# A hand-fed instruction list replaced by another search of the same list, in a fused attention and MLP layer

## The chip, the cores and the metric

The kernel runs on one core of one Trainium2 chip. The metric is the device time of one execution in microseconds (us). Lower is better. Three runs of the kernel before gave 302.27, 302.45 and 305.53, so the median is 302.45.

## The reference, cut to what matters

The input `A_x` has 2048 rows of 640 numbers in bf16. A layer norm, an attention and a residual are followed by a second layer norm, an MLP and another residual.

```python
def _A_ref(x, wq, wk, wv, wo, beta):          # H = 32 heads, Dh = 20, N = 4 segments, L = 512
    q, k, v = heads(x @ wq), heads(x @ wk), heads(x @ wv)       # [1, 32, 4, 512, 20]
    phi = lambda t: jnp.where(t > 0, t + 1.0, jnp.exp(t))
    for s in range(N):
        logits = einsum('bhqd,bhkd->bhqk', qs, ks) * Dh ** -0.5 + mask
        p = softmax(logits);  a_dot = einsum('bhqk,bhkd->bhqd', p, vs)
        pq = phi(qs);  num = einsum('bhld,bhde->bhle', pq, M)
        den = einsum('bhld,bhd->bhl', pq, z)[..., None] + 1e-06
        o = g * num / den + (1.0 - g) * a_dot
        pk = phi(ks)
        M = M + einsum('bhld,bhle->bhde', pk, vs);  z = z + pk summed over l
    return o @ wo

h  = x + _A_ref(layernorm(x), wq, wk, wv, wo, beta)
h2 = h + silu(layernorm(h) @ w1) @ w2         # w1 640 x 1728, w2 1728 x 640
```

## The kernel before, in words

The work is cut into four segments of 512 rows (0 to 3), and a segment into four blocks of 128 rows. All of it is declared as nearly 1,500 named tasks, and each task belongs to one engine. `Graph.schedule` walks a written list, the string `ORDER`, and hands the tasks to their engines in just that order. Every engine, and each of the two DMA-issuing queues (SyncE's, called SP here, and ScalarE's), then works in order. A task that has to wait holds up all that follows it on its engine. An entry is `name/engine:slots`: the engine letter (A ScalarE, D VectorE, G GpSimd, S SyncE) is given where there is a choice, and the slots are the buffers or PSUM banks it takes. `Tracker.add` derives the semaphore waits from reads and writes, buffers included. The list was made by a planner that has its own costs; only the finished list is in the kernel.

The names that the text uses, with the line that their instructions show in the profile:

- `x0`, `x1`, `x2`, `x4`, `x8`, `x12` (L577) load rows; `w_q`, `w_k0`, `w_w1_0` to `w_w1_4` and so on (L580) load weights; a `w_w1` part is 432 KB.
- `n1_st`, `n1_r`, `n1_ap` (L745, L760 to L766, L772): statistics, reciprocal root and application of the first layer norm of a block. Blocks 4 to 7 are segment 1.
- `n1_tp`, `n1_te` (L781, L790): the transpose of segment 0 by TensorE and its eviction by ScalarE. Later segments use DMA transposes, `n1_tr` (L796), issued by SyncE.
- `re_wq0` to `re_wk4` (L697, on ScalarE L695) copy the weights of q and k into a padded layout. These are copies in the head.
- `pr` and `qe` (L859, L867 or L868): a projection to q or k, and its eviction. In segment 0 each is done in two halves, `x` and `y`.
- `vt00` to `vt011` (L899): twelve small SBUF to SBUF transfers that gather head rows left over from the first five groups, so that groups 5 to 7 exist. Group 5 to 7 scores of segment 0 (`qk7x0` first) wait for all twelve.
- `qk`, `e`, `mk` (L936, L947, L958): scores on TensorE, their exponential on ScalarE, the causal mask on GpSimd. `av` and `oe` (L979, L994): probabilities times values, and the eviction; `tn` and `nm` (L1012, L1025 and L1027): transpose and division.
- `v` and `ve` (L824, L834 or L835): the value projection and eviction. `ex`, `pha`, `phb` (L874, L881, L887): the feature map. `kt` (L1093) and `mz` (L1101): transpose of the feature map by DMA, and the memory update.
- `ot`, `wo`, `rs` (L1154, L1162, L1170): transpose by DMA, output projection, residual. `h1`, `th`, `s` (L1197, L1206, L1212) and `h2`, `o` (L1239, L1252): the MLP. `out` (L1257) stores rows.
- `fill34`, `fill17`, `fill3` (L617): matmuls of zeros that only keep TensorE busy. `vpad0` and `vpad1` (L624, L625): GpSimd memsets of padding beside the values; `mt`, `mta`, `mtb`, `mm`, `mzc`: small GpSimd tasks that make masks.

Of the kernel before, what the change touches and what calls it, by code (L numbers as in the profile page):

```python
# [324 lines left out]
D = 640  # L325
# [50 lines left out]
n1_st8:6 e1yb2 mk1yb_0 n1_tr6 mk1yb_256 phb011 oe4x/A:1 qk7x0:0 e7x2:2 e7x0 mk7x_0 n1_tr7 v02:4 ve02/A tn4x:6 av1x:7
oe1x/D:1 n1_ap11:2 nm4x:0 mk7x_256 n1_r8/G n1_ap9:0 pha031:1 qk5x0:0 e5x2:0 v11:4 e5x0 mk5x_0 mk5x_256 qk6x0:0 e6x0:1
ve11/D:1 tn2x:7 av7x:6 oe7x/D:0 tn1x:4 nm1x:3 nm2x:1 e6x2 mk6x_0 fill3:5 av3x:5 oe3x/A:1 mk6x_256 tn7x:6 nm7x:2
qk0ya0:0 e0ya2:5 av5x:4 oe5x/D:0 mz00:5 ma00/D:0 mb00:0 e0ya0 kt01:1 tn3x:7 nm3x:1 av6x:6 oe6x/D:1 qk1ya0:2 e1ya2:0
tn5x:7 nm5x:3 tn6x:6 nm6x:0 ot1:0 phb031 ot0 e1ya0 n1_st10:0 n1_r10/D v10:0 ve10/A qk2ya0:4 e2ya0:2 av0y:2 oe0y/D:1  # L380
mz02:3 ma02/D:3 v12:0 ve12/D e2ya2 qk2yb0:2 e2yb0:1 n1_ap10:1 w_w2_0/S mb02:0 wo1:6 rs1 e2yb2 mk2yb_0 n2_st1:5
qk3ya0:0 e3ya2:3 wo0:4 mk2yb_256 tn0y:6 nm0y:1 rs0 n2_r1/G n2_ap1:3 kt04:0 n2_tr1:0 av1y:7 oe1y/D:0 e3ya0 qk4ya0:0
pr101:6 qe101/D:0 e4ya2:4 n2_st0:3 n2_r0/G v13:4 ve13/D e4ya0 pha101:2 ex101:2 n2_ap0:3 n2_tr0 qk3yb0:0 pr120:7
e3yb2:5 e3yb0 qk4yb0:2 w_w2_1/S e4yb2:0 e4yb0 mk4yb_0 mk3yb_0 mk4yb_256 mk3yb_256 qe120/D:0 ex120:0 phb101 pha120:0
av2y:6 pr100:0 qk5ya0:2 e5ya2:2 oe2y/D:1 qe100/D tn2y:7 nm2y:2 pr121:1 qe121/D pha121:0 pha100:0 e5ya0 n1_ap8:3
# [929 lines left out]
```

## Time and profile before

| What | Value |
|---|---|
| median of three runs | 302.45 us |
| profiled execution, its own time | 302.91 us |
| its span, first to last instruction | 301.2 us |
| granted clock, mean | 0.999 |
| TensorE matmuls busy | 291.1 us (97%) |
| VectorE busy | 222.4 us (74%) |
| ScalarE busy | 221.2 us (73%) |
| GpSimd busy | 140.5 us (47%) |
| HBM read, written | 10.41 MB, 2.62 MB |

The table adds up over very different stages. In the first ten microseconds all engines wait for loads. From 10 to 45 us segment 0 is brought up. From 45 us to about 260 us attention of one segment runs beside the MLP of the one before, and from 260 us on only the MLP of segment 3 is left. A busy share of an engine in the table is therefore an average and bounds nothing by itself.

### The profile page before, as it was taken

The page shows a single profiled execution, that of the slowest core. Times are in us where ns is not written, and L with a number is a line of the kernel's source. Part 1 is how long each engine was busy: PE and PEld are TensorE (multiplying, and loading weights), DVE is VectorE, ACT ScalarE, POOL GpSimd, SP SyncE. Part 2 cuts the span into 40 slices and gives each one's busy share as a digit, 9 for nine tenths or more (in the row PEclk, how much of TensorE's full clock was granted, in tenths as well). Part 3 has the DMA queues.
Part 4 walks back from the last instruction along what each step waited for, and adds up shares of the span by engine and source line. Part 5 has one row for each costly group of instructions (what it writes and reads, how often), then busy time and mean ns, then how long its engine had stood idle before and what let it go on. Part 6 is the DMA issues. An engine that isn't in the chain of part 4 may idle for free.

```text
span 301.2 us, 7561 instructions
## 1 busy us (share of the span) xinstructions
PE 291.1 (97%) x3027; PEld 172.6 (57%) x3027; DVE 222.4 (74%) x519; ACT 221.2 (73%) x315; POOL 140.5 (47%) x271
## 2 busy tenths in 40 slices
PE   8899699999999999999999999999999999999996
PEld 6675355454655555656644544566565457764574
DVE  5999788878559789889679885758847778735613
ACT  2998798999997999999679989886787840004500
POOL 4799632534645556754645446662774621200000
PEclk9999999999999999999999999999999999999999
DMA  7999525315473200361441300243120022330001
GB/s 258 362 359 135 96 58 131 89 22 168 83 91 88 59 20 10 51 94 26 100 137 39 71 14 20 39 86 77 46 65 24 2 44 46 87 87 2 0 30 59
DMA packets 48738, 24.66 MB, mean 82 GB/s; under 512 B 39168, under 2 KB 47616, under 8 KB 48704
## 3 DMA queue, kind: packets, MB, share of 16 engines
q1 hardware_dynamic: 46604, 21.64, 31.4%
q10 hardware_dynamic: 2100, 2.55, 3.0%
q8 instruction: 24, 0.39, 0.5%
q14 instruction: 10, 0.08, 0.1%
HBM read 10.41 MB, written 2.62 MB: 43 GB/s over the span
## 4 chain that ended last, share of the span: by engine, by line
PE 81%; DVE 6%; ACT 5%; DMA 3%; SPq 2%; issue 1%; POOL 0%; ACTq 0%; DVEq 0%
PE ps_all L1239 20%; PE ps_all L1197 18%; PE ps_all L859 12%; PE ps_all L1162 8%; PE ps_all L936 7%; PE ps_all L824 6%; PE ps_all L979 5%; ACT PT L947 3%; SPq L899 2%; DMA x_tok<-in_A_x_dram 2%; PE ps_all L1008 2%; PE ps_all L1101 2%; DMA w_sb<-w_sb 2%; PE ps_all L1012 1%; PE ps_all L1191 1%
## 5 line engine op out<-in xcount | busy, mean ns | idle before, releaser
L947 ACT ACTIVATE PT<-ps_all 128x1024 bf16<-128x1024 f32 (+1 forms) x168 | 157.0, 993 | 19.5 <-PE ps_all L936 15.9
L958 POOL TENSOR_SCALAR_AFFINE_SELECT PT<-PT 128x512 bf16<-128x512 bf16 x128 | 81.8, 648 | 58.8 <-ACT PT L947 56.2
L1239 PE MATMUL ps_all<-w_sb,sT 128*128 128x320 bf16 (+2 forms) x462 | 64.8, 295 | 0.0
L1197 PE MATMUL ps_all<-hT,w_sb 128*128 128x512 bf16 (+1 forms) x325 | 62.8, 337 | 0.0
L1206 ACT ACTIVATE th<-ps_all 128x512 f32<-128x512 f32 (+2 forms) x70 | 34.4, 516 | 35.4 <-PE ps_all L1197 27.2
L1239 PEld LDWEIGHTS ps_all<-w_sb,sT 128*128 128x128 bf16 x462 | 43.3, 98 | 18.2 <-issue 2.4
L1212 DVE SCALAR_TENSOR_TENSOR sT<-th,ps_all 128x512 bf16<-128x512 f32 (+2 forms) x70 | 38.1, 560 | 18.0 <-ACT th L1206 17.2
L1197 PEld LDWEIGHTS ps_all<-hT,w_sb 128*128 128x128 bf16 x325 | 29.9, 98 | 25.3 <-issue 2.4
L766 POOL TENSOR_TENSOR rst<-rst,eps_c 128x1 f32<-128x1 f32 x32 | 18.6, 582 | 26.6 <-DVE rst L760 24.8
L1252 DVE SCALAR_TENSOR_TENSOR x_tok<-ps_all,x_tok 128x640 bf16<-128x640 f32 (+3 forms) x18 | 13.4, 747 | 22.9 <-PE ps_all L1239 22.9
L745 DVE BATCH_NORM_STATS2 stt<-x_tok 128x6 f32<-128x320 bf16 x62 | 27.2, 484 | 2.9 <-DMA x_tok<-in_A_x_dram 2.6
L1162 PE MATMUL ps_all<-wo_sb,oT 128*128 128x320 bf16 x160 | 24.1, 299 | 0.4 <-DVE x_tok L1252 0.4
L979 PE MATMUL ps_all<-PT,Vx 128*32 128x256 bf16 (+3 forms) x576 | 23.3, 287 | 0.4 <-DVE Vx L835 0.4
L1053 POOL TENSOR_TENSOR otok<-on 128x320 bf16<-128x320 bf16 x24 | 19.3, 805 | 9.1 <-DVE on L1045 9.1
L868 DVE CAST QK<-ps_all 128x512 bf16<-128x512 f32 x24 | 16.4, 688 | 6.7 <-PE ps_all L859 6.3
L994 DVE TENSOR_SCALAR oTs<-ps_all,lsc 128x512 bf16<-128x512 f32 (+1 forms) x31 | 18.9, 624 | 2.7 <-PE ps_all L979 2.6
L1045 DVE TENSOR_TENSOR on<-ps_all,rd 128x640 bf16<-128x640 f32 x24 | 19.8, 824 | 0.8
L1162 PEld LDWEIGHTS ps_all<-wo_sb,oT 128*128 128x128 bf16 x160 | 14.9, 98 | 7.7 <-issue 2.4
L859 PE MATMUL ps_all<-xT,wkr 128*128 128x512 bf16 x75 | 18.7, 380 | 0.0
L824 PE MATMUL ps_all<-wv_sb,xT 128*128 128x320 bf16 x120 | 18.3, 299 | 0.3 <-ACT Vx L834 0.3
L859 PE MATMUL ps_all<-xT,wqr 128*128 128x512 bf16 x75 | 18.5, 380 | 0.0
L979 PEld LDWEIGHTS ps_all<-PT,Vx 128*32 128x32 bf16 x576 | 12.3, 96 | 10.3 <-issue 3.9
(88 smaller groups left out, 344.9 us busy)
## 6 DMA issues: line engine op xcount, KB each, us to landing
w_sb<-in_B_w_dram SPq DMA_DIRECT2D x5, 432.0 KB, 11.0
x_tok<-in_A_x_dram SPq DMA_DIRECT2D x3, 640.0 KB, 10.3
w_sb<-in_B_w_dram SPq DMA_DIRECT2D x3, 480.0 KB, 3.8
out_dram<-x_tok SPq DMA_DIRECT2D x9, 160.0 KB, 1.8
out_dram<-x_tok ACTq DMA_DIRECT2D x6, 160.0 KB, 1.9
sT<-in_A_wq_dram SPq DMA_DIRECT2D x1, 800.0 KB, 6.3
wo_sb<-in_A_wo_dram SPq DMA_DIRECT2D x1, 800.0 KB, 12.5
QKV<-QK SPq DMA_DIRECT2D x11, 72.0 KB
```

Source lines behind the costliest of these rows:

```text
L745: T.add(DV, lambda e, hh=hh: e.bn_stats(out=stt[:, s, 6 * hh:6 * hh + 6], in_=xb[:, 320 * hh:320 * hh + 320]), reads=R((xa, xsub)), writes ...
L824: fns.append(lambda e, c=c, hh=hh: e.matmul(bank(ps, hh)[:, 0:320], lhsT=xT_[:, c, 128 * i:128 * i + 128], rhs=wv_sb[:, c, 320 * hh:320 * ...
L859: fns = [lambda e, kc=kc: e.matmul(bank(ps)[:, lo:hi], lhsT=wt[:, kc, c, :], rhs=xT_[:, kc, lo:hi], start=(kc == 0), stop=(kc == NC - 1)) ...
L936: fns.append(lambda e, j=j, o=o, r=r, q0=q0, q1=q1, qa=qa, ka=ka: e.matmul(ps_all[:, o:o + q1 - q0], lhsT=ka[32 * r:32 * r + DH, 128 * j:1 ...
L947: T.add(AC, lambda e: e.activation(out=pt[:, pta.slot, q0:q0 + 2, 0:width], in_=sc3[:, b0:b0 + 2, 0:width], func=ACT.Exp, scale=SCALE), re ...
L958: T.add(PO, lambda e: e.affine_select(out=v, in_=v, pattern=[[0, 4], [1, 128]], compare_op=ALU.is_ge, fill=0.0, base=0, channel_multiplier ...
L979: fns.append(lambda e, j=j, r=r, h=h, pa=pa, pt=pt, co=co, q0=q0, ji=ji: e.matmul(bank(po)[32 * r:32 * r + 32, q0:hi], lhsT=Vx[:, vx.slot, ...
L1162: fns.append(lambda e, c=c, hh=hh: e.matmul(bank(ps, hh)[:, 0:320], lhsT=oT[:, c, 128 * i:128 * i + 128], rhs=wo_sb[:, c, 320 * hh:320 * h ...
L1197: fns = [lambda e, c=c: e.matmul(bank(ps)[:, lo:hi], lhsT=w1_sb[:, c, 128 * f:128 * f + 128], rhs=hT[:, c, lo:hi], start=(c == 0), stop=(c ...
L1206: T.add(AC, lambda e: e.activation(out=th[:, tha.slot, lo:hi], in_=bank(ps)[:, lo:hi], func=ACT.Tanh, scale=0.5), reads=R((ps, [0])), writ ...
L1212: T.add(DV, lambda e: e.scalar_tensor_tensor(out=sT[:, f, lo:hi], in0=th[:, tha.slot, lo:hi], scalar=1.0, in1=bank(ps)[:, lo:hi], op0=ALU. ...
L1239: fns.append(lambda e, f=f, t0=t0, fr=fr, hh=hh, n=n: e.matmul(bank(pa, hh)[:, 0:n], lhsT=sT[:, f, t0:t0 + 128], rhs=w2_sb[:, fr, c0 + 320 ...
```

## The change

Only the string `ORDER` is different; no task is added or taken away, apart from two more matmuls of zeros in the first filler (`fill36` for `fill34`). Every engine's order changes in places, and some evictions move between ScalarE and VectorE. What is different in the head, engine by engine:

- SyncE's queue. Before: `x0 w_q w_k0 w_wv0 x4 w_wo beta w_w2_4 x8 w_w1_3 w_w1_2 w_w1_0 w_w2_5 w_w1_4 w_w1_1 kt00 vt04 vt02 vt010 vt011 vt08 vt03 vt00 vt05 n1_tr5 n1_tr4 kt02 n1_tr6 n1_tr7 kt01 ot1 ot0 w_w2_0 kt04`. After: the same up to `w_w2_4`, then `w_w1_3 w_w2_5 w_w1_0 w_w1_4 x8 w_w1_2 vt08 vt05 vt01 vt010 vt011 vt03 vt04 vt09 n1_tr5 kt02 kt00 n1_tr4 n1_tr7 n1_tr6 w_w1_1 kt04 ot1 ot0 kt01`.
- ScalarE issues `vt02 vt07 vt06 vt00` instead of `vt01 vt07 vt06 vt09`, and later also `w_w2_0` and `x12`.
- GpSimd does both `vpad` tasks at its start, no longer beside the head copies.
- VectorE applies `n1_ap1` ahead of `n1_st2`. `n1_st10` comes ahead of `ve11`; `n1_ap5` comes behind `phb021`.
- `kt00` goes from the place ahead of the `vt` transfers to one behind them.

The rows of the list around these steps:

```diff
-n1_st0/D:1 mtb0 n1_r0/G mm2 w_wv0 x4:1,2,4,6 w_wo:0 beta w_w2_4 x8/S:8,9,10,11 w_w1_3:0 w_w1_2 w_w1_0 n1_st1/D:6
-n1_ap0:0 n1_r1/G w_w2_5 n1_st2/D:2 n1_r2/D n1_ap1:1 n1_r3/G mt2 mm4 mtb1 mm3 mt3 vpad1 mta2 mtb2 mm10 mm9 re_wq0/D:0
-n1_ap2:3 mm7 mm0 mm5 re_wq1/D mta3 mtb3 vpad0 n1_ap3:2 w_w1_4 w_w1_1 re_wk0/D:0 re_wq2/D mm1 re_wk3/D re_wk2/D mm8 mm6
...
-mzc6 lsc1 mzc3 mzc1 mk1x_0 mzc5 mzc7 phb001 kt00:1 pr041y:7 pr030x:5 pr031x:4 qe031x/A mzc4 epsg1 qe041y/A:0 qe030x/A
...
-ex011:2 pha021:1 mk4x_256 pr020y:5 pr010y:4 v00:6 qe020y/D qe010y/D vt03/S vt00/S vt06/A n1_st11:2 n1_r11/G ve00/D:0
-n1_st9:1 n1_ap6:1 pha011:2 n1_r9/G vt05/S qk0yb0:2 e0yb2:4 e0yb0 mk0yb_0 mk0yb_256 vt09/A n1_tr5:0 v01:0 ve01/A v03:6
...
+halfc:0 x1:3 vpad0 zpad mt2 epsc x0:7 iota sel w_q:0 x2:5,0 vpad1 mt1 w_k1 w_k0 w_wv0:0 w_wv1 x4:1,2,4,6 mta2 w2z/D:0
+mta1 mtb1 mtb2 w_wo:0 beta w_w2_4 mm7 warm n1_st0/D:1,0 n1_st1/D:6 mm5 mm1 n1_r0/G n1_r1/D n1_ap0:0 n1_ap1:1 w_w1_3:0
+w_w2_5 w_w1_0 w_w1_4 x8/S:8,9,10,11 n1_st2/D:2 n1_r2/D n1_st3/A:0 n1_r3/G re_wq0/D:0 mm10 mt0 re_wq1/D mta0 mtb0 mm0
...
+phb041 qe011y/D qe010y/D n1_st11:2 n1_r11/G vt03/S qk4x0:0 e4x2:5 e4x0 mk4x_0 v00:6 ve00/D:0 vt06/A qk0yb0:2 e0yb0:4
+mk4x_256 phb021 n1_ap5:0 vt00/A vt04/S vt09/S n1_st9:1 n1_tr5:0 kt02:0 v01:0 kt00:1 e0yb2 n1_r9/G mk0yb_0 v03:6 ve03/D
+mk0yb_256 n1_tr4 ve01/A ex011:2 n1_tr7 n1_tr6 w_w1_1 qk1yb0:2 av0x:0 oe0x/D:1 av2x:1 oe2x/D:0 e1yb0:6 av4x:6 tn0x:7
+nm0x:0 e1yb2 n1_st8:6 oe4x/A:1 mk1yb_0 mk1yb_256 n1_ap9:0 pha031:1 qk7x0:0 e7x0:2 e7x2 mk7x_0 v02:4 tn4x:6 nm4x:0
+av1x:7 oe1x/D:1 mk7x_256 ve02/A qk5x0:0 e5x0:0 e5x2 ex031:0 n1_r8/G n1_st10:0 v11:4 mk5x_0 mk5x_256 pha011:2 qk6x0:0
```

More of the change, by code (lines that the diff above doesn't have):

```diff
@@ L376 @@
[L376 to L385, printed above, removed]
```

180 lines of the change are left out of this document (94 added, 86 removed).

## The prediction

> **What bounds the kernel now.** I read the page, then TensorE's waits, then the head in order of time, engine by engine. The page:
>
> ```profile
> PE 291.1 (97%) x3027; PEld 172.6 (57%) x3027; DVE 222.4 (74%) x519; ACT 221.2 (73%) x315; POOL 140.5 (47%) x271
> ```
>
> TensorE (PE) has work for 97% of the span, so 301.2 - 291.1 = 10.1 us of it are idle, and no order of the list can win more than these, the matmuls of zeros, and the small delays inside what counts as busy. In TensorE's waits, the ones that a list can influence are:
>
> ```profile
> PE ps_all L936 <- DMA w_sb<-w_sb: 1.6, 1, 1.6
> PE ps_all L1012 <- DVE Vx L835: 0.8, 1, 0.8
> PE ps_all L936 <- DVE oTs L994: 0.7, 1, 0.7
> PE ps_all L1162 <- DVE x_tok L1252: 0.4, 1, 0.4
> ```
>
> The two longest lie in the head, as TensorE's order of time shows (start, length, and in brackets the idle time and what ended it):
>
> ```profile
> 30.02 0.25 PE L1012 MATMUL ps_all<-ident,oTs 128*128 128x84 bf16 x2
> 31.89 0.34 PE L936 MATMUL ps_all<-w_sb 20*128 20x256 bf16 x8 [1.61 <-DMA w_sb<-w_sb]
> 34.59 1.52 PE L824 MATMUL ps_all<-wv_sb,xT 128*128 128x320 bf16 x10 [0.25 <-ACT Vx L834]
> 37.63 0.25 PE L1012 MATMUL ps_all<-ident,oTs 128*128 128x84 bf16 x2 [0.79 <-DVE Vx L835]
> ```
>
> At 31.89 `qk7x0` waits for the last `vt` transfer, at 37.63 `tn1x` for `ve11`. ScalarE (ACT) has its only long gaps of the first 90 us around the same places, because its exponentials come from these scores:
>
> ```profile
> 26.10 0.81 ACT L947 ACTIVATE PT<-ps_all 128x768 bf16<-128x768 f32 x1 [1.34 <-DVE stt L745]
> 32.28 1.51 ACT L947 ACTIVATE PT<-ps_all 128x768 bf16<-128x768 f32 x2 [1.43 <-PE ps_all L936]
> 36.43 1.51 ACT L947 ACTIVATE PT<-ps_all 128x768 bf16<-128x768 f32 x2 [0.54 <-PE ps_all L936]
> 38.61 0.47 ACT L992 ACTIVATE oTs<-ps_all,lsc 128x256 bf16<-128x256 f32 x1 [0.67 <-DVE rd L1025]
> ```
>
> That is 4.0 us. In the table of stretches ScalarE is then busy 9.70 of 10 us (50 to 60) and 19.96 of 20 (60 to 80), and TensorE 10.00 and 19.24. Two engines that are this full make nothing good later: what the head loses, the end has lost, and what the head wins is kept unless the new list adds waits. The chain that ended last shows what the loss at 31.89 hangs on:
>
> ```profile
> 23.70 1.85 SPq L899
> 25.66 0.79 SPq L899
> 26.49 0.74 SPq L899
> 27.28 4.52 DMA w_sb<-w_sb
> 31.80 0.09 issue
> ```
>
> `vt03`, the sixth of eight issues on SyncE, waits for `qe010y`, VectorE's copy that ends at 25.21. The eighth, `vt05`, is issued by 27.97 and lands at 31.80.
>
> **The change, part by part.** Nothing new is computed, so every price is a shift of rows.
>
> *The vt transfers.* The same three issues stand behind `qe010y` on SyncE as before, and `kt00` is gone from ahead of them. The start hangs on VectorE (DVE). Ahead of `qe010y` the list drops six tasks (four 256-wide evictions, `n1_ap1`, `n1_ap5`) and takes six of the same kinds (four evictions, `n1_ap4`, `n1_ap6`), so the work is equal. One price differs:
>
> ```profile
> 11.49 1.59 DVE L697 COPY wkr<-sT 128x400 bf16<-128x400 bf16 x5
> 13.00 1.17 DVE L697 COPY wqr<-sT 128x400 bf16<-128x400 bf16 x6
> ```
>
> Six copies take 1.17, so five should take 0.98; the slow five ran beside `vpad1` (POOL L624 at 11.44, 0.73). With `vpad1` gone to the start, where VectorE waits for `x0` until 3.76, they win 1.59 - 0.98 = 0.6. `qe010y` then ends near 24.6, the last issue near 27.4. From there to landing the trace gives 3.8 us with `n1_tr5` issued right behind (28.01); the nearest row without a transpose behind it is a store of 160 KB, 1.8 us from issue to landing. So landing lies between 29.2 and 31.2. TensorE itself is ready at 30.36 before (`oe2x` ends) and, with VectorE 0.6 ahead and `ap5` and `phb021` (0.44 + 0.62) where `ap6`, `pha011`, `ap4` (0.39 + 0.28 + 0.44) stood, at 29.7. The wait of 31.89 ends between 29.7 and 31.3: a win of 0.6 to 2.2. In the new list `n1_ap5` is ready just when SyncE is through with `vt09`, so `n1_tr5` is behind the transfers again, and I take 1.2, nearer to the row that has the transpose.
>
> [...]
>
> *From there to qk0ya0.* Before, 31.89 to 38.61 is 6.7 us. ScalarE's work in between is `e7` 1.45, `ve02` 0.65, `e5` 1.4 and `e6` 1.4, from the distances of its rows, with `ex031` (0.52) moved in from earlier; with 0.4 to the first that is 5.8. On VectorE `n1_st10` (1.02, from L745 and L748) is now ahead of `ve11`, while `phb021`, `phb011` and `n1_ap11` (0.62 + 0.37 + 0.80) leave that stretch. Bounds -0.3 (if `n1_st10` makes `ve11` later) and +0.9; I take 0.5.
>
> *Ahead of 25 us.* The two matmuls of zeros cost 2 x 0.15 (5.21 / 34), hidden behind `n1_st3`, which holds ScalarE until 8.94; uncovered 0.3. On ScalarE `re_wk1` (0.72) and `n1_te3` (0.58) now precede the first exponentials, which start about 0.6 later, but the four evictions gone to VectorE equal the four that come, so by `e4` ScalarE has done the same work, with `ex021` in the place of `ex031`. I take 0, bounds -0.6 and +0.3. `vt06` still blocks ScalarE until `qe010y`, and moves with it.
>
> *w_w1_1 and x8.* From 3 to 24 us the loads run at 360 GB/s, so the 432 KB moved away end them 1.2 us sooner. `x8`, issued at about 11.5 instead of 8.86, lands in 10.3 (the page's median), at 22; `n1_st11` reads it at 25: 3 us of cover. `w_w1_1` is issued behind six transposes of 1.2 to 1.4 each, at about 36, and lands by 47 even with the 11.0 of the head; the first `h1` of the chain is at 58.7. Its issue (0.4) is ahead of `kt04`, `ot1` and `ot0`, but `ot1` waits for `nm6x`, whose row ends near 42. `n1_tr5` serves `v11`, `n1_tr4` and `n1_tr6` serve `v10` and `v12` at 41 and 43.7; the row of transposes is through by 36, 5 us of cover. `kt02` lands near 30.5, and `pha031`, which needs its buffer, comes near 31: cover 0.5, and 1 us if that is gone. All 0.
>
> *Behind 45 us.* Orders and buffers change in places: `qk8b0` takes a bank freed by `oe6y` instead of `oe7y` (0.7 in the waits), `wo2` one freed by `nm8` instead of `o1` (0.4); further waits of 0.3 and 0.2 stand in the list. `w_w2_0` and `x12` go to ScalarE; `x12` waits there for a store to land, which held SyncE 1.4 us, at a place where ScalarE idles for more. Old waits may go and new ones come: I take 0, bounds +1.6 and -1.6. The tail is the same.
>
> *Sum.* 1.2 + 0.5 = 1.7. The profiled execution took 302.91 (span 301.2 and 1.7 around it), so 301.2; from the median of the runs, 302.45, it is 300.75. I forecast 301.0.
>
> **Rivals.**
>
> 1. No gain: the transposes keep the vt transfers back. Six transposes now stand in a row behind `vt09`, where before two did. For it: the 3.8 us of `vt05`, against 1.8 for a store. Against: SyncE cannot issue `n1_tr5` before `n1_ap5`. Release stays at 31.9 and the 0.5 remains or not: 302.5.
> 2. Slower: VectorE, not the transfers, sets the head. The copies `re_wk3` and `re_wk4` show records of 1.23 and 1.19; if they last that long wherever they stand, and not because of `vpad`, adding up the records of the new order from 7.25 on puts `qe010y` at 26.4, 1.2 later than 25.21. `vt06` blocks ScalarE that long, and `vt03` starts later by it. Release at 33.1, and every exponential behind it 1.2 late: 302.9 + 1.2 = 304.1, and up to 305.7 with the 1.6 of late waits. It decides from `qe010y` ending past 25.8. Against: the six copies of 1.17.
> 3. More gain: transfers land as the store does, 2.2 + 0.9, and the waits at `qk8b0` and `wo2` go (1.1): 302.9 - 4.2 = 298.7.
>
> **How the numbers follow.** Forecast 0.40, no gain 0.25, slower 0.18, more gain 0.17. A measurement of this kernel can tell about 1%, some 3 us, from no change. Faster by over 1% (below 299.4) is nearly all of the third rival and a little of the forecast: 0.19. Slower by over 1% (above 305.5) is the part of the second with new waits behind 45 us, and a list whose late waits alone add more than I bounded: 0.15. Within 1%: 0.66. The range reaches to the third rival, 298.7, and to 304.4, the second without all its late waits. The forecast's own range is 299.7 to 302.3.
>
> **What would show it.** Right: TensorE's wait for `w_sb<-w_sb` falls from 1.6 to under 1, `qk7x0` starts between 29.7 and 31.3, the five `wkr` copies take about 1.0, and ScalarE's gap before 26.10 shrinks by about 0.6. Wrong: that wait stays or grows (first rival), `qe010y` ends past 25.8 (second), or new waits of over 0.5 stand behind 45 us on TensorE or ScalarE.

## The result, and the profile after

The changed kernel took 305.2 us in the median of 20 runs, the kernel before 302.44 in the median of 20 beside them; the ratio is 1.005, with a 95% interval of 1.0027 to 1.0073. The forecast was 301.0 with a range of 298.7 to 304.4, so it missed by 4.2 us and the range did not reach far enough. (The ratio is not that of the medians, which is 1.009; it leaves out one run of the kernel before, at 307.94, as a slow one.) The runs of the changed kernel fall in two groups, 7 from 302.9 to 304.3 and 13 from 305.1 to 305.8. The runs of the kernel before spread too, from 301.7 to 307.9, but 12 of the 20 lie below 302.9. This spread turned out to be part of the answer.

The profiled execution took 305.39 us (span 303.7), so it belongs to the upper group. The page:

```profile
PE 290.5 (96%) x3006; PEld 173.2 (57%) x3029; DVE 220.9 (73%) x517; ACT 222.6 (73%) x317; POOL 141.4 (47%) x271
```

TensorE has the same work, and 303.7 - 290.5 = 13.2 us outside of it instead of 10.1. But the trace lacks 23 of the 3029 matmuls, and the 13.2 count these holes too (the small waits for "issue" are holes), so the two can't be compared: two complete traces of the changed list with one edit each, `m1_after_narrow_masks` and `d4_after_fill48` below, have 9.2 and 9.8 us outside, less than the kernel before. TensorE's waits, of those that a list can influence:

```profile
PE ps_all L1012 <- DVE oTs L994: 0.8, 1, 0.8
PE ps_all L1101 <- DMA phiKt<-phiK: 0.8, 1, 0.8
...
PE ps_all L617 <- DVE Vx L835: 0.7, 1, 0.7
PE ps_all L936 <- DVE w_sb L868: 0.6, 1, 0.6
PE ps_all L859 <- ACT hT L790: 0.5, 1, 0.5
...
PE ps_all L936 <- DMA w_sb<-w_sb: 0.4, 1, 0.4
```

The wait for the `vt` transfers, 1.6 before, is down to 0.4, as forecast. The 0.7 at L617 is the old wait for `ve11` (0.8 before, met by the filler ahead of `tn1x` now). Of the other four three are new, that at L936 was 0.3 before, and the first two lie far behind the head. TensorE's order of time in the head:

```profile
31.61 0.34 PE L936 MATMUL ps_all<-w_sb 20*128 20x256 bf16 x8 [0.37 <-DMA w_sb<-w_sb]
37.26 0.50 PE L617 MATMUL ps_all<-zpad 128*128 128x256 bf16 x3 [0.70 <-DVE Vx L835]
```

`qk7x0` starts at 31.61, only 0.28 sooner than before, since TensorE itself arrives so late that there is little left to wait for. ScalarE shows the same in its gaps:

```profile
26.91 0.81 ACT L947 ACTIVATE PT<-ps_all 128x768 bf16<-128x768 f32 x1 [1.18 <-DVE stt L745]
32.01 1.51 ACT L947 ACTIVATE PT<-ps_all 128x768 bf16<-128x768 f32 x2 [0.19 <-PE ps_all L936]
38.24 0.47 ACT L992 ACTIVATE oTs<-ps_all,lsc 128x256 bf16<-128x256 f32 x1 [0.57 <-DVE rd L1025]
```

The gap of 1.43 is down to 0.19, that of 1.34 is not closed, and its end has moved from 26.10 to 26.91. Where the 2.5 us between the two profiled executions went is seen best by following the start of the same tasks. The table also has a second execution of the changed kernel (it is the first experiment of the second group below), which fell in the lower group:

| start of (us) | before | after | after, second execution |
|---|---|---|---|
| `e0ya0`, end of the head | 39.98 | 39.61 (-0.37) | 37.34 (-2.64) |
| `e7yb0` | 66.45 | 66.98 (+0.53) | 64.72 (-1.73) |
| `e21b0` | 155.91 | 155.94 (+0.03) | 153.68 (-2.23) |
| end of the span | 301.2 | 303.7 (+2.5) | 301.1 (-0.1) |

So there are three things to explain. The head is better by 0.4 us in one execution and by 2.6 in the other, from the same program. Between 40 and 66 us 0.9 is lost in both (0.5 of it comes back by 156). Behind 156 us 2.2 to 2.4 is lost in both. The forecast had -1.7 for the first and 0 for the two others.

The chain that ended last shows the two later places. The first is at 50 us:

```profile
50.26 4.17 DMA hT<-xn_rot
...
54.53 0.45 DVE xn_rot L772
54.98 0.61 DVE QK L868
55.58 0.02 issue
55.61 0.47 DVE phiQ L881
56.08 0.40 DVE oTs L994
56.48 0.05 issue
56.53 0.25 PE ps_all L1012 x2
```

`n2_tr1`, a transpose by DMA issued by SyncE at 50.26, takes 4.17 us to land; the same transpose took 2.6 before. VectorE's `n2_ap0` at 54.53 waits for its buffer (0.85 us), all that is behind it on VectorE is late, and TensorE waits 0.85 at 56.53. What is new is that ScalarE issues `w_w2_0` (640 KB) at 49.44, 0.8 us ahead of the transpose; SyncE issued it at 45.53 before, and it landed 4.4 us later, at 49.9, 0.6 ahead of the transpose (50.54).

The second is at 154 us, in the chain and on VectorE:

```profile
154.49 6.41 DMA phiKt<-phiK
160.91 0.02 issue
160.93 0.29 DVE phiK L881
```

```profile
157.49 0.69 DVE L1212 SCALAR_TENSOR_TENSOR sT<-th,ps_all 128x512 bf16<-128x512 f32 x1 [0.49 <-ACT th L1206]
160.93 0.29 DVE L881 TENSOR_SCALAR phiK<-QK 128x512 bf16<-128x512 bf16 x1 [2.75 <-DMA phiKt<-phiK]
161.14 0.68 DVE L1212 SCALAR_TENSOR_TENSOR sT<-th,ps_all 128x512 bf16<-128x512 f32 x1
```

`pha241` overwrites the buffer that the transpose `kt23` reads, so it waits for `kt23` to land. Before, VectorE had `s1_4_0` and `n1_st12` ahead of it and came to it 0.2 us early. In the new list it is ahead of both, and VectorE stands for 2.75 us with `s1_4_0` behind it, for which ScalarE waits 1.80 us and TensorE after it. `kt23` is slow in both kernels (most transposes of this line, L1093, land in 2.3 to 2.4 us), and in both `x12` (640 KB) is issued 0.4 us ahead of it. The lists of DMA issues from 152 to 158 us (before, then after; the last number is the time from issue to landing):

```profile
x_tok<-in_A_x_dram SPq DMA_DIRECT2D x1, 640.0 KB, 4.6
...
phiKt<-phiK SPq DMA_TRANSPOSE x1, 6.2
```

```profile
x_tok<-in_A_x_dram ACTq DMA_DIRECT2D x1, 640.0 KB, 6.3
...
phiKt<-phiK SPq DMA_TRANSPOSE x1, 6.4
```

### The profile page after: what moved, and what is told of

The parts are those of the page before. It is cut to its first block, busy times and chain, and to the rows that moved or that the text cites. A ratio compares the mean times of both kernels' runs of the same rounds, so it can differ in the third digit from the quotient of the medians.

```text
span 303.7 us, 7526 instructions
## 1 busy us (share of the span) xinstructions
PE 290.5 (96%) x3006; PEld 173.2 (57%) x3029; DVE 220.9 (73%) x517; ACT 222.6 (73%) x317; POOL 141.4 (47%) x271
## 4 chain that ended last, share of the span: by engine, by line
PE 74%; DVE 14%; ACT 5%; DMA 5%; issue 1%; POOL 0%; DVEq 0%; SPq 0%
PE ps_all L1239 19%; PE ps_all L1197 15%; PE ps_all L859 9%; PE ps_all L1162 6%; PE ps_all L936 6%; PE ps_all L979 5%; PE ps_all L824 5%; ACT PT L947 3%; DMA phiKt<-phiK 3%; PE ps_all L617 3%; DVE stt L745 3%; PE ps_all L1008 2%; PE ps_all L1012 1%; DMA hT<-xn_rot 1%; PE ps_all L1101 1%
## 5 line engine op out<-in xcount | busy, mean ns | idle before, releaser
L1197 PE MATMUL ps_all<-hT,w_sb 128*128 128x512 bf16 (+1 forms) x315 | 61.1, 336 | 1.4 <-issue 0.7
L1197 PEld LDWEIGHTS ps_all<-hT,w_sb 128*128 128x128 bf16 x325 | 29.7, 98 | 25.5 <-issue 2.7
L772 DVE TENSOR_SCALAR xn_rot<-x_tok,mvt,rst 128x640 bf16<-128x640 bf16 x32 | 14.9, 473 | 5.0 <-POOL rst L766 4.0
L859 PE MATMUL ps_all<-xT,wkr 128*128 128x512 bf16 x67 | 16.9, 380 | 1.0 <-issue 0.8
L859 PE MATMUL ps_all<-xT,wqr 128*128 128x512 bf16 x70 | 17.4, 380 | 0.5 <-issue 0.3
```

Of the source, the lines that this page charges most:

```text
L859: fns = [lambda e, kc=kc: e.matmul(bank(ps)[:, lo:hi], lhsT=wt[:, kc, c, :], rhs=xT_[:, kc, lo:hi], start=(kc == 0), stop=(kc == NC - 1)) ...
L1197: fns = [lambda e, c=c: e.matmul(bank(ps)[:, lo:hi], lhsT=w1_sb[:, c, 128 * f:128 * f + 128], rhs=hT[:, c, lo:hi], start=(c == 0), stop=(c ...
```

## The experiments

Sixteen runs in four groups of four; the kernels of a group shared a chip and the runs of the kernel before. The table gives the median of their times, the ratio to the kernel before with its interval, and from the one profiled execution of each: when TensorE's pace doubles (a 128x256 matmul of zeros takes 0.213 us up to that moment and 0.108 from there on), when `n1_tp0` starts, and TensorE's idle time in three stretches (no matmul record running, us). The expectations call that moment the doubling of TensorE's clock, which is the author's reading: the granted clock reads 1.00 on both sides of it, in the trace of before (3.85) and in that of after (6.35). Times of one profiled execution and the medians are different things, as the two groups teach. A median is over 12 runs, but over 7 for `d4_after_fill48` and 6 for `m3_all_four_again`.

| kernel | median (us) | ratio, 95% | pace doubles | `n1_tp0` | 25 to 45 | 45 to 60 | 152 to 170 |
|---|---|---|---|---|---|---|---|
| before | 302.44 | 1 | 3.85 | 6.33 | 3.69 | 0.01 | 0.20 |
| after | 305.2 | 1.005 (1.0027 to 1.0073) | 6.35 | 7.55 | 2.69 | 1.17 | 1.95 |
| e1_w20_sync | 302.67 | 1.0005 (0.9978 to 1.0033) | 5.55 | 7.19 | 2.93 | 0.43 | 1.96 |
| e2_x12_sync_ahead | 303.01 | 0.9995 (0.9964 to 1.0025) | 5.73 | 7.26 | 2.92 | 1.17 | 1.26 |
| e3_x12_behind_kt23 | 304.43 | 1.0029 (0.9999 to 1.0058) | 6.16 | 7.47 | 2.65 | 1.17 | 1.76 |
| e4_pha241_later | 303.84 | 1.0014 (0.9986 to 1.0042) | 4.86 | 6.83 | 1.78 | 1.17 | 1.01 |
| c1_after_again | 304.38 | 1.003 (0.9996 to 1.0063) | 3.85 | 6.51 | 1.43 | 1.18 | 1.84 |
| c2_before_fill24 | 303.26 | 0.9975 (0.9936 to 1.0014) | 5.35 | 6.11 | 2.92 | 0.32 | 0.46 |
| c3_after_fill24 | 303.42 | 1.0013 (0.9979 to 1.0046) | 3.85 | 6.14 | 1.43 | 1.17 | 1.84 |
| c4_all_four | 301.32 | 0.9937 (0.9902 to 0.9973) | 4.71 | 6.25 | 1.43 | 0.44 | 0.64 |
| d1_before_w20_scalar | 303.68 | 1.0024 (0.9996 to 1.0052) | 6.61 | 7.48 | 3.41 | 1.15 | 0.20 |
| d2_before_pha241_early | 304.58 | 1.006 (1.0034 to 1.0086) | 4.67 | 6.53 | 2.59 | 0.01 | 1.16 |
| d3_before_w11_late | 302.28 | 0.9961 (0.9933 to 0.9989) | 7.05 | 7.73 | 4.36 | 0.01 | 0.20 |
| d4_after_fill48 | 305.94 | 1.0091 (1.0054 to 1.0127) | 4.92 | 8.23 | 2.06 | 0.86 | 1.57 |
| m1_after_narrow_masks | 303.76 | 0.9999 (0.9974 to 1.0024) | 5.09 | 6.95 | 1.27 | 0.85 | 1.57 |
| m2_before_narrow_masks | 303.62 | 1.0001 (0.9973 to 1.0029) | 6.41 | 7.39 | 3.08 | 0.01 | 0.20 |
| m3_all_four_again | 300.76 | 0.991 (0.9877 to 0.9943) | 5.96 | 6.43 | 1.43 | 0.14 | 0.26 |
| m4_three_fill36 | 302.28 | 0.9955 (0.9926 to 0.9985) | 4.28 | 6.6 | 1.43 | 0.14 | 0.26 |

The median of the kernel before was 302.44, 303.34, 303.59, 303.24 and 303.22 beside the changed kernel and the four groups, so a median is compared with its own group's; the columns at the right do not suffer from that. They suffer from the holes: the traces of `after`, of the first group and of the second lack 23 matmuls each, which adds about 0.3 us to each of the last two columns. The complete traces with the changed list in these stretches, `m1` and `d4`, have 0.85 and 1.57.

Each run also has its mean granted clock on record, and this matters for the medians. Of the 129 runs of the kernel before beside the four groups, 55 show 0.994 or less, with a median of 304.45; the other 74 show 0.999 or 1.000, called full clock below, and have a median of 302.57. With the changed kernel's head, 5 of 141 runs show 0.994, and none of the 32 runs of the changed kernel itself; their median is 305.1, so at full clock the change costs 2.5 us. What such a run has in it is shown in the fourth group.

### First group: the two later waits, undone in the changed kernel

`e1_w20_sync`, the 640 KB away from the transpose:

```diff
-... e4ya2:4 w_w2_0/A e4ya0 ...
+... qk2yb0:2 e2yb0:1 w_w2_0/S ve12/D ...
```

> The changed kernel, with the load of w_w2_0 (640 KB) issued by SyncE again, at about 45 us as before, and not by ScalarE at 49.44, 0.8 us ahead of the transpose n2_tr1. Theory A (the load shares the DMA engines with the transpose): n2_tr1 lands in about 2.6 us, not 4.17, VectorE's 0.85 at 54.53 and TensorE's 0.85 at 56.53 are gone, and TensorE at 58 us is 0.3 ahead of the kernel before instead of 0.6 behind; what is left of it at the end is between nothing and 0.9: 304.3 to 305.2. Rival (the waits at 54 to 57 us come from the order on VectorE): the two waits stay and the time is the changed kernel's, 305.2.

`n2_tr1` landed in 2.6 us, VectorE came to `n2_ap0` at 53.48 without a wait, TensorE's 0.85 was gone, and the idle time between 45 and 60 us fell from 1.17 to 0.43. `e7yb0` started at 66.14, 0.3 ahead of the kernel before. The times at this place are those of theory A; in what way the load holds the transpose back, no run shows. The median, 302.67, came lower than expected, because 7 of the 12 runs were in the lower group.

`e2_x12_sync_ahead`, `x12` where it was before:

```diff
-... s1_10_0:0 qk21b0:3 x12/A tn16:0 ...
+... o3 out3/S x12/S av18:7 ...
```

> The changed kernel, with x12 (640 KB) on SyncE again, behind out3 and ahead of the transpose kt23, as before. Theory A (VectorE stands at pha241, and TensorE at mz23, until kt23 has landed, and kt23 lands late because it shares the DMA engines with x12): x12 is issued at 153.5 and not at 154.06, kt23 lands at about 160.2 and not at 160.9, VectorE still stands some 2 us there; 0.7 of the 2.2 us come back: 304.5, in one group and not two. Rival B (the order behind 158 us costs the 2.2 us by itself, whatever the transfers do): 305.2. Rival C (x12 on ScalarE's queue is the whole of the loss): 303.0.

`x12` was issued at 153.58 (154.06 in the changed kernel), `kt23` landed at 159.8, and VectorE still stood 1.60 us. The idle time from 152 to 170 us fell by 0.7, from 1.95 to 1.26. The median, 303.01, is below the 304.5 expected and is that of rival C by chance, as 8 of the 12 runs were in the lower group; VectorE's wait, which stayed, speaks against rival C. So `x12` on ScalarE's queue makes over a third of the loss: there it stands behind ScalarE's work and goes out 0.5 us later, which the prediction had put at nothing. There were still two groups, 302.0 to 303.5 and 304.3 to 304.5, so they have another cause.

`e3_x12_behind_kt23`, the transpose ahead of the load:

```diff
-... s1_10_0:0 qk21b0:3 x12/A tn16:0 ...
+... kt23:1 x12/S mb14:0 ...
```

> The changed kernel, with x12 on SyncE right behind the transpose kt23, so that kt23 always goes first. Theory A: kt23 lands about 2.6 us after its issue, near 157.1, VectorE and TensorE do not stand for it, and all runs are at 303.0, the lower of the two groups in which the changed kernel's runs fall. n1_st12, which reads x12, comes at about 160 then and has x12 by 159.6. Rival B (the order itself): 305.2. Rival D (x12 later makes n1_st12 and the transposes of segment 3 late): 305 or more, with VectorE's wait at L745 on x12 instead.

A miss. VectorE's row at the place where the cost went:

```profile
158.73 0.42 DVE L881 TENSOR_SCALAR phiK<-QK 128x512 bf16<-128x512 bf16 x1 [0.69 <-DMA phiKt<-phiK]
...
161.51 0.89 DVE L745 BATCH_NORM_STATS2 stt<-x_tok 128x6 f32<-128x320 bf16 x2 [1.43 <-DMA x_tok<-in_A_x_dram]
```

The wait for `kt23` shrank to 0.69 and `n1_st12` then waited 1.43 for `x12`, 2.1 us in place of 2.75: that is rival D. Whichever of the two transfers goes first, the other one has a reader on VectorE that is due. With the load 1.2 us behind it, `kt23` still took 4.3 us.

`e4_pha241_later`, VectorE's order alone:

```diff
-... s1_7_0 pha241:0 th1_4_0:0 s1_4_0 ... phb241 ... n1_st12:0 th1_12_0:0 ...
+... s1_7_0 th1_4_0:0 s1_4_0 ... n1_st12:0 pha241:0 phb241 th1_12_0:0 ...
```

> The changed kernel, with pha241 and phb241 on VectorE behind s1_4_0 and n1_st12, as in the list before; no transfer moves. Theory A: kt23 lands at 160.9 as in the changed kernel, VectorE no longer stands 2.75 us, TensorE still waits about 0.8 at mz23: 303.5 to 304.3. Rival B (the loss sits in the transfers or elsewhere, and VectorE's order does not matter): 305.2.

The idle time from 152 to 170 us fell from 1.95 to 1.01 with no transfer moved, and the median came to 303.84, within the expected interval. VectorE's order makes over half of this loss.

### Second group: why one program has two heads

The profile of `e4_pha241_later` had an oddity: its head was 1.4 us ahead of the three others, though the four lists are the same up to 45 us. The first difference stands at the very start. The changed kernel's first profile and, below it, its second (TensorE; L617 are the matmuls of zeros, L781 is `n1_tp0`):

```profile
2.14 5.57 PE L617 MATMUL ps_all<-zpad 128*128 128x256 bf16 x31
7.55 0.44 PE L781 MATMUL ps_all<-ident,xn_rot 128*128 128x128 bf16 x5
```

```profile
2.15 4.39 PE L617 MATMUL ps_all<-zpad 128*128 128x256 bf16 x31
6.51 0.45 PE L781 MATMUL ps_all<-ident,xn_rot 128*128 128x128 bf16 x5
```

The same 31 matmuls take 5.57 us in one and 4.39 in the other. Record by record, a matmul of zeros takes 0.213 us up to some moment and 0.108 from there on, and this moment differs from execution to execution, from 3.85 to 7.05 us in the table. `n1_tp0`, whose input is ready at 6.4, stands behind all 36.

`c1_after_again`, no edit, as the control on this chip:

> The changed kernel once more, without an edit, beside the three that follow. Its times fell in two groups, 302.9 to 303.5 and 305.1 to 305.8, two thirds of them in the upper one. Theory F (filler): the matmuls of zeros take 0.213 us each until TensorE's clock doubles and 0.108 after it, the doubling comes at another moment in every execution (3.9 to 6.4 us in the profiles so far), and n1_tp0 stands behind all 36 of them. Then this profile has either a doubling before 5 us and a time in the lower group, or one after 5.4 and a time in the upper group. Rival L (loads): the groups come from HBM loads that land late, and the two do not go together.

The profile has its doubling at 3.85 and 302.85 us, the lower group. Of all profiles in the table that have the changed list's head, those that start `n1_tp0` by 6.95 have `e0ya0` at 37.3 to 38.3, and those that start it at 7.19 or later at 39.5 to 39.7, with nothing between.

`c2_before_fill24` and `c3_after_fill24`, the filler shortened:

```diff
-fill34:0
+fill24:0
```

```diff
-fill36:0
+fill24:0
```

> The kernel before, with 24 matmuls of zeros in the first filler instead of 34, so that they end by 1.1 + 24 x 0.213 = 6.2 us whenever the clock doubles, and n1_ap0 ends at 6.28. Theory F: the upper part of the kernel's times (303.4 to 305.5) goes away, the median falls from 302.4 or 303.3 to about 302.2, all below 303.2. Rival L: the spread stays 302 to 305. Rival W (the filler is what keeps the clock up): TensorE falls back to the slow clock in the gap, and the median rises by 1 or more.

> The changed kernel, with 24 matmuls of zeros in the first filler instead of 36. Theory F: n1_tp0 starts at 6.4 to 6.9 in every execution and not at up to 7.55; the exponential e0ya0 starts near 38.2 as in the profile with the early doubling, not at 39.5; all times fall in the lower group, 302.9 to 303.9, median 303.3, which is 1.9 under the changed kernel's 305.2. Rival L: two groups as before. Rival W: median above 305.2.

In the changed kernel 9 of 12 runs were at 302.8 to 303.6, and 3 between 305.0 and 306.7, where without the edit 19 of 32 runs were at 304.9 or more: theory F holds for the most part. In the kernel before it does not: 6 runs at 301.9 to 302.8, 6 at 303.8 or more, as without it. What makes the kernel before spread is something else: 5 of these 6 show a granted clock of 0.994. Rival W fell for the median: TensorE idled 0.9 us after the short filler in the profile of `c3_after_fill24`, and the mean granted clock of that execution is 1.000. But one of its 12 runs, the one at 306.66, has 0.994, and so have 2 of the next one's, against 2 of 111 runs with the changed head and the longer filler; so few can't settle whether the short filler makes such runs more frequent.

`c4_all_four`, the four edits together:

> The changed kernel with four edits: 24 matmuls of zeros in the first filler, w_w2_0 on SyncE at 45 us, x12 on SyncE behind out3, and pha241 and phb241 behind n1_st12. Theory: the four are additive where they lie in different stages: 303.3 (the lower group) - 0.7 (w_w2_0) - 1.3 to 1.5 (pha241 with x12 ahead; the two share one loss and do not add fully) = 301.2, so about 1 below the kernel before (302.2) and level with it or better where that is at its best. Rival: the later stages take back what these give (a later wait takes the place of each), 302.5 to 303.

301.32 us, where 301.2 was expected: the edits add up. At full clock the median is 301.25, and 302.47 for the kernel before beside it.

### Third group: the parts alone, in the kernel before, and the filler made longer

`d1_before_w20_scalar`:

```diff
-... n1_ap10:1 w_w2_0/S mb02:0 ...
+... qe101/D:0 e4ya2:4 w_w2_0/A n2_st0:3 ...
```

> The kernel before, with one part of the change alone: w_w2_0 is issued by ScalarE behind e4ya2 (near 49.8 us), as in the changed list, and not by SyncE at 45.53. Theory A (the 640 KB share the DMA engines with the transpose n2_tr1, and VectorE's n2_ap0 waits for its buffer): n2_tr1 lands 1.5 us later than before, TensorE's idle time between 45 and 60 us rises from 0.0 or 0.3 to about 1.0, the time by 0.6 to 0.8. Rival (it takes the changed kernel's order on VectorE as well): no wait over 0.3 there, same time.

The two rows of the changed kernel appear in the kernel before, on VectorE and on TensorE:

```profile
54.99 0.45 DVE L772 TENSOR_SCALAR xn_rot<-x_tok,mvt,rst 128x640 bf16<-128x640 bf16 x1 [1.14 <-DMA hT<-xn_rot]
```

```profile
57.45 0.25 PE L1012 MATMUL ps_all<-ident,oTs 128*128 128x84 bf16 x2 [1.15 <-DVE oTs L994]
```

TensorE's idle time from 45 to 60 us went from 0.01 to 1.15. The lowest time was 303.03, against 301.9 beside it; the medians differ by 0.4, and by 0.9 at full clock (303.56 against 302.64).

`d2_before_pha241_early`:

```diff
-... s1_7_0 s1_4_0 n1_st12:0 ... pha241:0 ...
+... s1_7_0 pha241:0 s1_4_0 n1_st12:0 ...
```

> The kernel before, with pha241 on VectorE ahead of s1_4_0 and n1_st12, as in the changed list; no transfer and no other task moves. Theory A (VectorE stands there until kt23 has landed): VectorE waits about 1.9 us for kt23, s1_4_0 ends near 161.0 and not at 158.95, TensorE's idle time between 152 and 170 us rises from 0.2 to between 1.0 and 1.6, the time by 1.0 to 1.5. Rival B (the order alone does nothing; it takes x12 on ScalarE): no change.

VectorE waited 2.06 us, `s1_4_0` ended at 160.9, the idle time from 152 to 170 us rose from 0.20 to 1.16, and the median by 1.3 (ratio 1.006, 1.0034 to 1.0086). At full clock, which 5 of its 12 runs have, it is 1.2 (303.87 against 302.64). One entry of a list, moved by two places on one engine, costs 0.4% of the time.

`d3_before_w11_late`, the later load of `w_w1_1` alone:

```diff
-... w_w1_4 w_w1_1 kt00:1 ...
+... n1_tr7 w_w1_1 v02:4 ...
```

> The kernel before, with the load of w_w1_1 (432 KB) moved on SyncE from ahead of kt00 to behind n1_tr7, the last transpose of segment 1. The theory gives it nothing, since the load has 10 us of cover: within 0.3 of the kernel before, and TensorE's wait for w_sb<-w_sb at 31.89 stays at 0.9 to 1.6. Rival G (the head's loads end 1.2 us sooner, so x8 and the vt transfers do too): 0.5 to 1.0 faster. Rival S (the load runs beside kt01 and the transposes of the attention output): 0.5 slower or more, with a wait of TensorE at L1101 or L1162.

302.28 against 303.24 beside it, ratio 0.9961 (0.9933 to 0.9989), so somewhat faster; 11 of the 12 runs lie at 301.75 to 303.2. Part of this is that only 1 of its 12 runs shows the lower granted clock, against 11 of 30 beside it; at full clock the medians are 302.14 and 302.64. Whether the edit has to do with either, 12 runs can't tell. The one that was profiled is the twelfth (304.33), and shows nothing of that gain but something else, on VectorE and on GpSimd:

```profile
24.75 2.33 DVE L881 TENSOR_SCALAR phiK<-w_sb 128x512 bf16<-128x512 bf16 x1
27.00 0.74 DVE L868 CAST w_sb<-ps_all 128x256 bf16<-128x256 f32 x2
```

```profile
23.36 3.57 POOL L958 TENSOR_SCALAR_AFFINE_SELECT PT<-PT 128x512 bf16<-128x512 bf16 x6
```

An instruction of 0.28 us (`pha021`) took 2.33, and ended at 27.08, 0.15 us after the last of six causal masks that GpSimd did in a row (26.93). The trace of before has the same meeting in a mild form, six masks from 22.59 on and the same instruction 2.6 times as long as alone:

```profile
23.81 0.74 DVE L881 TENSOR_SCALAR phiK<-w_sb 128x512 bf16<-128x512 bf16 x1
```

`d4_after_fill48`:

```diff
-fill36:0
+fill48:0
```

> The changed kernel, with 48 matmuls of zeros in the first filler instead of 36: the suspected cost made longer. Theory F: even when TensorE's clock doubles at 3.85 us, 13 slow and 35 fast ones end at 7.6, so n1_tp0 starts at 7.6 or later in every execution, e0ya0 at 39.5 or later, and there is no lower group: median 305.3 to 306.3, none below 304.5. Rival L (the groups have another cause): two groups as before, median within 0.4 of the changed kernel's.

As theory F has it: `n1_tp0` at 8.23 with the pace doubled at 4.92, `e0ya0` at 39.66, no run below 305.17. But `e0ya0` is hardly later than the 39.61 of the changed kernel's first profile, where `n1_tp0` came 0.7 sooner. In the profiles the head has two places to be in, and the filler only decides between them.

### Fourth group: what the filler sets off

The rows of VectorE between the two (the changed kernel's first profile, then its second) say what the step is. L643 is `lsc3`, L772 `n1_ap4`, L887 `phb041`, and the last row holds `qe011y` and `qe010y`:

```profile
23.26 0.63 DVE L643 TENSOR_SCALAR lsc<-lsc 128x8 f32<-128x8 f32 x1
23.80 0.85 DVE L772 TENSOR_SCALAR xn_rot<-x_tok,mvt,rst 128x640 bf16<-128x640 bf16 x1
24.58 0.85 DVE L887 TENSOR_TENSOR phiK<-phiK,ex 128x512 bf16<-128x512 bf16 x1
25.35 0.74 DVE L868 CAST w_sb<-ps_all 128x256 bf16<-128x256 f32 x2
```

```profile
22.36 0.16 DVE L643 TENSOR_SCALAR lsc<-lsc 128x8 f32<-128x8 f32 x1
22.43 0.44 DVE L772 TENSOR_SCALAR xn_rot<-x_tok,mvt,rst 128x640 bf16<-128x640 bf16 x1
22.78 0.41 DVE L887 TENSOR_TENSOR phiK<-phiK,ex 128x512 bf16<-128x512 bf16 x1
23.12 0.74 DVE L868 CAST w_sb<-ps_all 128x256 bf16<-128x256 f32 x2
```

```profile
23.23 2.69 POOL L958 TENSOR_SCALAR_AFFINE_SELECT PT<-PT 128x512 bf16<-128x512 bf16 x4
```

GpSimd's masks `mk2x` and `mk3x` start at 23.23 in the slow head (the last row) and at 22.99 in the fast one. VectorE is through with the three SBUF instructions by 23.2 in the fast head. In the slow one it is 0.9 us later and meets the masks, and the three take 2.33 instead of 1.01. The copies from PSUM in the row below take 0.74 either way, and in the fast head too masks run beside them (22.99 to 25.46). So 0.9 becomes 2.2, and `vt06`, which holds ScalarE, waits for it.

`m1_after_narrow_masks` and `m2_before_narrow_masks`:

```diff
-                def e_mask(eng, co=co):
-                    v = pt[:, pta.slot, :, co:co + 128]
+                def e_mask(eng, co=co, mw=8 if name.endswith("x") else 128):
+                    v = pt[:, pta.slot, :, co:co + mw]
...
-                        out=v, in_=v, pattern=[[0, 4], [1, 128]], compare_op=ALU.is_ge, fill=0.0,
+                        out=v, in_=v, pattern=[[0, 4], [1, mw]], compare_op=ALU.is_ge, fill=0.0,
```

> The changed kernel, with the masks of the first score groups (mk0x to mk7x) on 8 columns instead of 128, so that GpSimd is free in the head; the causal mask of those scores is mostly left out. Theory P (VectorE's instructions stand while a mask of 0.64 us runs on GpSimd): n1_ap4 and phb041 take 0.44 and 0.42 and not 0.85 each, qe010y ends at 24.2 to 24.8 even when TensorE's clock doubles late, e0ya0 starts by 38.4, and the upper group is gone: median 302.7 to 303.4. Rival (the masks are not to blame, the late filler alone is): two groups, the upper one at 305.

> The kernel before, with the same narrow masks in the head. Theory P: pha021 on VectorE takes 0.28 us in every execution (0.74 in the profile of before, 2.33 in the slowest profile so far), and the upper group of before (303.4 to 305.5) is gone: all below 302.9, median 301.7 to 302.2. Rival: two groups as before.

In the changed kernel all 12 runs lie between 303.0 and 304.0: with the narrow masks the upper group is gone (`n1_ap4` and `phb041` took 0.44 and 0.42 in the profile), though the filler is as long as before, and what is left of the spread, 1.0, is about the filler's own (`n1_tp0` at 6.51 or 7.55). Its median of 303.76 is 0.4 above the expected interval. In the kernel before the rival held: two groups, 3 runs below 302.3 and 9 from 303.1 to 304.8. In the profiled one VectorE's rows were short (`pha021` took 0.24) and TensorE still waited 2.33 us for `qk7x0`. What the upper group has instead is the clock: 8 of its 9 runs show 0.994, and the three below 302.3 show 1.000. The profiled run is one of the 8, the only profile of all with such a clock, and it shows where the loss lies (the row of TensorE, then stretches of 1 us; the third number from the right is the granted clock):

```profile
32.48 0.35 PE L936 MATMUL ps_all<-w_sb 20*128 20x256 bf16 x8 [2.33 <-DVE mvt L748]
```

```profile
33.00:34.00 1.00, 1.00 (x9) 0.65 (x8) 0.00 (x0) 1.00 (x2) 0.00 (x0) 0.85 1.21 75
34.00:35.00 1.00, 1.00 (x10) 0.59 (x11) 0.00 (x0) 0.61 (x2) 0.48 (x3) 0.50 0.81 159
35.00:36.00 1.00, 1.00 (x18) 0.33 (x11) 0.56 (x2) 0.67 (x2) 0.69 (x2) 0.50 0.75 152
36.00:37.00 1.00, 1.00 (x6) 0.54 (x4) 0.97 (x4) 1.00 (x2) 0.00 (x0) 0.50 0.07 12
37.00:38.00 1.00, 1.00 (x14) 0.56 (x12) 0.37 (x3) 0.32 (x1) 0.46 (x2) 0.94 0.00 0
```

About 1.2 us after the long wait TensorE's granted clock falls to 0.50 for 3.4 us, from 33.7 to 37.1, and eight scores take 0.51 us there instead of 0.34. At half the clock that is 1.7 us of its work, an estimate; by the rows, `qk6x0` starts 5.08 us after `v02` instead of 3.87 in the trace of before. 1.7 of 302.4 is 0.6%, which is what a mean of 0.994 lacks; that the other runs of 0.994 have one such stretch each is an estimate from this one profile. The medians of the kernel before with and without it, 304.45 and 302.57, are 1.9 apart. This is a large part of the spread of the kernel before, and the changed list, in which the wait for `qk7x0` is short (0.37 in its first profile), is nearly free of it. That the wait sets the stretch off is the author's guess and not shown: in the profile of `d3_before_w11_late` TensorE waited 2.07 us up to 27.9 and kept its clock (eight scores at 31.0 took 0.34, the mean is 1.000). The 74 runs at full clock still reach from 301.85 to 304.77, and the masks make such times too (the profile of `d3`, 304.33 at full clock).

`m3_all_four_again` and `m4_three_fill36`:

> The version with the four edits once more: 24 matmuls of zeros, w_w2_0 on SyncE, x12 on SyncE, pha241 and phb241 behind n1_st12. If the gain is real, the median is again 301.2 to 301.6 and the ratio to the kernel before 0.991 to 0.997; if the first result was a lucky mix of the groups, the median is 302 to 303.

> The same version with 36 matmuls of zeros again, so three edits of the four. Theory F: two groups return, the lower near 301.0 and the upper near 303, with about as many runs in the upper as in the changed kernel: median 302 to 303. Rival: the filler does not matter once the later waits are gone: 301.3.

The version with four edits is ahead of both kernels again: 300.76 us, 0.4 below the expected, ratio 0.991 (0.9877 to 0.9943). All of its runs are at full clock, and there the kernel before has 302.56, so 1.8 us are won with the clock set aside. Its profile has a late doubling, 5.96, and yet the fast head, `e0ya0` at 37.37. With 36 matmuls of zeros the times reach from 300.6 to 303.2 without a gap, with one at 305.7 (clock 0.994), and the median is 302.28, as theory F has it: the filler alone is worth 1.5 us in the median (6 runs against 12), and nothing in the best run. One loss is left: `e21b0` starts 2.9 us sooner than in the kernel before and the span ends only 2.2 sooner, and no run looks for these 0.7 us.

## Why the prediction was wrong, by its own steps

*The vt transfers, +1.2.* The mechanism was right, but in the profiled execution its sign came by luck: TensorE's wait fell from 1.6 to 0.4 because TensorE came later, and the release moved by 0.28 only. Six transposes in a row behind the transfers held them back no longer than two did: from the start of the last issue on SyncE, 27.8, to TensorE's start at 31.6 are 3.8 us, where the chain of before had 4.52. So the first rival did not happen; whether transposes hold the transfers back at all, no run shows. The ten `wkr` copies took 1.76 us, so five took 0.9, as forecast, and the second rival's reason, long copies, was wrong. Its sign was there all the same: `qe010y` ended at 26.09, past its 25.8, for the reason in the fourth group. In the second execution `qe010y` ended at 23.9 and `qk7x0` started at 29.85, inside the forecast 29.7 to 31.3, and the head gained 2.64, more than the 1.7 of the sum. So the sum of the head describes one place of the two, and the trace of before, a single execution, could not show that there are two. The change also won something that no step had priced: the runs with a granted clock of 0.994 or less went from 55 of 129 to none of 32. That this comes from the shorter wait is the author's guess, not shown.

*Ahead of 25 us, 0.* This is the first step that failed: "the two matmuls of zeros cost 2 x 0.15, hidden behind `n1_st3`". They cost 0.213 each up to the moment when the pace doubles. And what counts is not the two that were added but that `n1_tp0` stands behind 36, so that it starts at 7.55 in the execution with the late doubling and at 6.51 in the other. The price per matmul, 5.21 / 34, had mixed both speeds. Why the moment differs, from 3.85 to 7.05 us in 18 executions, no run shows. With the two speeds in the records of before, the filler should have had a range in the sum: at most 36 x 0.213 = 7.7 us, an estimate with no doubling at all, where the two executions took 6.5 and 5.4.

*VectorE's durations.* The prediction added up the records of before as if they belonged to the instructions. `n1_ap4`, 0.44 there, took 0.85 beside a mask, and it had itself seen such a pair (the copies beside `vpad1`) and taken it for the padding alone. The 0.74 of `pha021` beside the masks in the trace of before was another. In the rows of the fourth group `n1_ap4` and `phb041` grew beside the masks, from 0.44 and 0.41 to 0.85 each, and the copies from PSUM kept their 0.74; why the one kind grew and the other did not, no run shows.

*From there to `qk0ya0`, +0.5.* In the profiled execution most of it was used up: `kt02` landed at 33.9 and not at 30.5, `pha031` waited 0.4 for it, and `fill3` ahead of `tn1x` waited 0.70 for `ve11`. The cover of 0.5 that the text gave to `kt02` was not there, since SyncE issued it at 30.66.

*Behind 45 us, 0.* This is the step that failed at the highest cost, and its bound of 1.6 did not hold it. The starts of the tasks give 0.9 us between 40 and 66 us and 2.2 to 2.4 behind 156. TensorE's idle time, in the complete traces, rose from 0.01 to 0.85 between 45 and 60 us and from 0.20 to 1.57 between 152 and 170, so by 2.2 in all. The prediction named both transfers, `w_w2_0` and `x12`, and asked only what ScalarE loses by issuing them. It did not ask which transposes they now run beside, nor who waits for those. "A place where ScalarE idles" was also wrong: `x12` stood 0.5 us behind ScalarE's work. And it did not walk VectorE's order at 158 us, where one entry had moved ahead of two others. `d1_before_w20_scalar` and `d2_before_pha241_early` show that each of these two does its damage alone, in the kernel before.

*w_w1_1, 0.* `d3_before_w11_late` gives 0.4% for it, and the interval excludes no change, but part of that is the clock of the runs beside it; its mechanism was not seen, as the profiled execution was not one of the typical ones.

*The tail* was the same, as forecast: TensorE's idle time from 220 us to the end is 2.5 us in every profile without holes, 2.4 of it behind the last matmul.

What stays open: what sets off the stretch at half clock that the clock of 55 of the 129 runs of the kernel before points to, what the runs at full clock differ in besides the masks, and the 0.7 us behind 156 us that are lost with all four edits too.

## What to carry to other kernels

When a load is moved to another queue, price it by what it now runs beside: the issue of 640 KB took 0.4 us, but the transpose next to it was 1.6 us late, and the next writer of that transpose's source stood in order ahead of work that was ready. A profile is one execution: a filler of fixed count, whose matmuls go from 0.213 to 0.108 us at a moment that differs from execution to execution (3.85 to 7.05 us here), and VectorE instructions that meet a row of GpSimd's masks (2.33 us for three instead of 1.01) stood behind two profiled executions of the same program at 302.85 and 305.39, so look at the spread of the runs, and at the granted clock of each, before trusting a sum to half a microsecond. And a list that is better in its best case is not better yet: the new head was worth 2.6 us, and three entries and a filler count kept it from being seen.

## What the runs showed of the hardware

- A 128x256 matmul of zeros took 0.213 us up to a moment and 0.108 from there on; the moment lay between 3.85 and 7.05 us in 18 executions, with the first matmul at 1.1. The granted clock reads 1.00 on both sides of it in the traces of before and after.
- In 79 of 189 runs with the head of before the mean granted clock was 0.994 or less. The one such run with a profile (`m2_before_narrow_masks`) had a granted clock of 0.50 on TensorE for 3.4 us, 1.2 us after a wait of 2.33, and eight scores took 0.51 us there instead of 0.34; another profile (`d3_before_w11_late`) kept the clock through a wait of 2.07.
- A VectorE instruction of 0.28 us (`pha021`), started at 24.75 beside six GpSimd masks in a row (23.36 to 26.93), took 2.33 and ended at 27.08. Beside another row of masks, 0.67 us each, two instructions took 0.85 each instead of 0.44 and 0.41, and two copies from PSUM took 0.74 as in the other head.
- A transpose by DMA of 2.6 us (`n2_tr1`) took 4.2 when a load of 640 KB was issued 0.8 us ahead on another queue. Another (`kt23`; its kind mostly takes 2.3 to 2.4) took 6.4 with the load 0.4 us ahead on another queue, and the load 6.3; 6.2 with the load 0.4 us ahead on the same queue, and the load 4.6; 5.3 with it 0.9 us ahead on the same queue, and the load 5.7; 4.3 with the load 1.2 us behind.
